# Loading and transposing one contraction block of x first, the next one behind the first weights, and moving one bank copy to VectorE

## The chip, the cores and the metric

The kernel runs on one core of a Trainium2 chip. The metric is device microseconds of one execution, so lower is better. A ratio below is always the mean time of one kernel's fast runs over the mean of the kernel before's fast runs of the same rounds on the same chip, with a 95% interval; it is therefore not quite the ratio of the medians that stand beside it. "By the clock" below means by these times; "the clock of TensorE" is the rate at which it works.

## The reference

```python
B, S, D, F = 32, 32, 1024, 3584        # bf16, x is 1024 tokens by 1024
def reference(x, w_gate, w_up, w_down):
    return (gelu(x @ w_gate) * (x @ w_up)) @ w_down     # tanh gelu
```

## The kernel before

A small recorder collects all operations, sorts those of each engine other than TensorE by an `at` value, works out the semaphores and emits five instruction streams. Most of the kernel (block products with sums of operands, Strassen-like) is not touched. What matters here is its first 12 us: the products of the first tokens with eight stripes of weights (four of gate, four of up), one contraction block of 128 at a time. TensorE needs x with the contraction on the partitions. Blocks 0 and 1 of x are loaded plainly and transposed by TensorE; later blocks come by transposing DMA.

```python
for n in [512] * 6 + [P] * 2:                      # warm-up matmuls, result unused
    mm(3, one[:, 0:P], one[:, 0:n], True, True)

NX = 2
for i, eng in enumerate(("sp", "act")):            # x, blocks 0 and 1 in one: rows of 512 B
    dma(eng, xn[:, 2 * i:2 * i + 2, :], x_r[:, 2 * i:2 * i + 2, 0:NX * P], 0, f"xn{i}")
# ...
for q in range(2):                                 # weights: gate on SP, up on ACT, block by block
    for k in range(NX):
        load_quad("sp", q, 0, k, k + 1)
        load_quad("act", q, 1, k, k + 1)
# ... transposing loads of x on SP, more weights on ACT ...
act(warm[:, 0:1], const0, GELU, 0)                 # brings the activation table in early
for k in range(NX):                                # eight transposes, four copies to SBUF
    for i, b in enumerate((6, 7) if k == 0 else (4, 5)):
        half = ps[:, b, 0:P].bitcast(BF16)
        for t in range(2):
            pr.add("pe", "transpose", half[:, t * P:(t + 1) * P], xn[:, 2 * i + t, k * P:(k + 1) * P], ident[:, :])
        pr.add("dve", "tensor_copy", xT[0][:, k, i * 256:(i + 1) * 256], half)
# ...
for k in range(NX):                                # first group: 8 products of block 0, 8 of block 1
    for j in range(2):
        for m in range(4):
            raw(m, j, k, 2 * m + j, k == 0)        # into PSUM bank 2m + j
            if k == NX - 1:                        # bank done: copied out, in turn by ScalarE and VectorE
                copy(("act", "dve")[m % 2], kept[m][:, j, :], bank(2 * m + j), 6.5 + 0.9 * j + 0.1 * m)
# ... the second group (m = 4 to 7) then fills the same eight banks, in the order 0 2 4 6 1 3 5 7
```

## Time and profile before

| | before |
|---|---|
| time, median of the first 3 runs | 271.86 us (271.35 to 272.02) |
| PE busy | 99% of the span |
| first product starts | 4.61 us |
| x lands (SP half, ACT half) | 3.25, 3.46 us |
| block-0 weights land (gate, up) | 4.03, 4.59 us |
| block-1 weights land (gate, up) | 6.74, 6.92 us |
| first product of block 1 | 7.32 us |
| first product of the second group | 9.04 us |

Landing times and starts of single matmuls are those recorded in the trace.

In the profile lines, PE is TensorE's matmuls, PEld its weight loads, DVE VectorE, ACT ScalarE and POOL GpSimd. `ps` is PSUM; `arena` holds the weights and transposed x; `hT` first holds x as loaded and later the copies of the banks. The page of the kernel before begins with the busy time of each engine:

```profile
PE 268.2 (99%) x1206; PEld 192.6 (71%) x1206; DVE 208.2 (77%) x246; ACT 136.1 (50%) x221; POOL 37.1 (14%) x23
```

The chain of waits of the kernel before, in order of time (start in us, length in us, what ran):

```profile
by line: PE ps L117 99.0%; DVE o L117 0.1%; issue 0.0%
...
0.77 3.79 PE ps L117 x16
4.56 0.05 issue
4.61 264.41 PE ps L117 x1190
...
```

The last line shown matters most: from 4.61 us on, 1190 matmuls follow one another and wait for nothing. What makes TensorE start later, do more, or wait once in the first microseconds is therefore added to the whole time.

The timeline of the kernel before up to 12.4 us, for TensorE, VectorE and ScalarE (start, length, engine, line, operation, output and inputs, count; in brackets the idle time before and what ended it):

```profile
0.77 2.93 PE L117 MATMUL ps<-const-bfloat16-1.0 128*128 128x512 bf16 x8 [0.77 <-PEq L632]
3.50 1.06 PE L117 MATMUL ps<-ident,hT 128*128 128x128 bf16 x8
4.61 8.05 PE L117 MATMUL ps<-arena 128*128 128x512 bf16 x32
...
3.95 0.93 DVE L117 COPY arena<-ps 128x256 bf16<-128x256 bf16 x4 [3.95 <-PE ps L117]
7.95 2.48 DVE L117 COPY hT<-ps 128x512 f32<-128x512 f32 x4 [3.06 <-PE ps L117]
...
5.25 1.28 ACT L117 ACT_TABLE_LOAD   x1 [5.25 <-issue]
7.73 1.57 ACT L117 ACTIVATE hT<-ps 128x512 f32<-128x512 f32 x3 [0.98 <-PE ps L117]
```

The warm-up lasts until 3.5 us, and x has just landed. All eight transposes follow at once. The products start when the first two copies are in SBUF. The copies that free the banks (output `hT`) are shared: four on VectorE, four on ScalarE. A matmul's own length overlaps with the next one's, so the pace has to be read from the starts: consecutive products of 512 columns start 0.427 us apart until 6.3 us and 0.216 us apart from 6.7 us on. The clock of TensorE doubled in between.

### The profile page before, as it was taken

What the parts mean: (1) busy time and instruction counts of PE and PEld (TensorE: products, weight loads), DVE (VectorE), ACT (ScalarE), POOL (GpSimd) and SP (SyncE); (2) the same over time, 40 slices, a digit from 0 to 9 for tenths busy, and PEclk for the clock granted to TensorE, in tenths of its full rate; (3) what the DMA queues carried; (4) which work ended last, traced back from release to release, by engine and by line L of the source; (5) the groups of instructions that cost most, each with busy time, mean ns of one, the idle gap of its engine ahead of it and who ended that gap; (6) DMA issues with size and microseconds to landing.
All of it is one profiled execution on the core that took longest, in us unless ns stands there. A gap on an engine that the chain in (4) does not pass through costs nothing.

```text
span 270.8 us, 3333 instructions
## 1 busy us (share of the span) xinstructions
PE 268.2 (99%) x1206; PEld 192.6 (71%) x1206; DVE 208.2 (77%) x246; ACT 136.1 (50%) x221; POOL 37.1 (14%) x23
## 2 busy tenths in 40 slices
PE   8999999999999999999999999999999999999997
PEld 4444448888888888888776776674458888888884
DVE  1338998998899889988764739379976999999921
ACT  2339877566756675667455554531220305057452
POOL 1000003123302330233344160000000000000000
DMA  6999970050492002971900070294010000002102
GB/s 205 205 316 204 280 188 4 13 141 0 116 291 60 0 0 80 254 251 51 263 0 0 0 247 27 65 351 129 0 39 19 4 0 0 0 0 80 58 21 97
DMA packets 45024, 27.47 MB, mean 101 GB/s; under 512 B 8656, under 2 KB 45008, under 8 KB 45008
## 3 DMA queue, kind: packets, MB, share of 16 engines
q1 hardware_dynamic: 42496, 25.04, 34.0%
q10 hardware_dynamic: 2512, 2.23, 3.3%
q8 instruction: 9, 0.15, 0.2%
q14 instruction: 7, 0.06, 0.1%
HBM read 23.33 MB, written 2.10 MB: 94 GB/s over the span
## 4 chain that ended last, share of the span: by engine, by line
PE 99%; DVE 0%; issue 0%
PE ps L117 99%; DVE o L117 0%
## 5 line engine op out<-in xcount | busy, mean ns | idle before, releaser
L117 PE MATMUL ps<-S,T 128*128 128x512 f32 x560 | 129.2, 391 | 0.0
L117 PEld LDWEIGHTS ps<-S,T 128*128 128x128 f32 x560 | 105.2, 188 | 22.3
L117 ACT ACTIVATE tmp<-ps 128x512 f32<-128x512 f32 x64 | 38.0, 596 | 51.7 <-PE ps L117 51.5
L117 POOL TENSOR_TENSOR T<-arena 128x1024 fp32r<-128x1024 bf16 x17 | 36.4, 2153 | 124.5 <-PE ps L117 81.7
L117 PE MATMUL ps<-T,S 128*128 128x512 f32 x224 | 51.3, 390 | 0.0
L117 DVE TENSOR_TENSOR T<-arena,T 128x1024 fp32r<-128x1024 bf16 x42 | 51.0, 1220 | 0.2
L117 PEld LDWEIGHTS ps<-T,S 128*128 128x128 f32 x224 | 42.1, 188 | 8.8
L117 ACT ACTIVATE ps<-ps 128x512 f32<-128x512 f32 x44 | 25.6, 584 | 37.0 <-PE ps L117 37.0
L117 DVE TENSOR_TENSOR hT<-tmp,ps 128x512 bf16<-128x512 f32 x56 | 37.0, 684 | 8.7 <-PE ps L117 6.7
L117 PE MATMUL ps<-arena 128*128 128x512 bf16 x192 | 43.5, 385 | 0.1
L117 DVE TENSOR_TENSOR tmp<-ps,tmp 128x512 f32<-128x512 f32 x28 | 19.4, 692 | 23.5 <-PE ps L117 23.5
L117 PEld LDWEIGHTS ps<-arena 128*128 128x128 bf16 x192 | 18.5, 99 | 23.7 <-issue 2.4
L117 DVE TENSOR_TENSOR T<-arena 128x1024 fp32r<-128x1024 bf16 x25 | 30.0, 1222 | 4.4 <-PE ps L117 4.3
L117 DVE TENSOR_TENSOR ps<-ps,tmp 128x512 f32<-128x512 f32 x32 | 22.3, 696 | 3.0 <-PE ps L117 3.0
L117 PE MATMUL ps<-arena,hT 128*128 128x512 bf16 (+2 forms) x126 | 24.6, 356 | 0.0
L117 PEld LDWEIGHTS ps<-arena,hT 128*128 128x128 bf16 x126 | 11.7, 98 | 12.7 <-issue 0.5
L117 ACT ACTIVATE tmp<-tmp 128x512 f32<-128x512 f32 x28 | 17.6, 632 | 2.4 <-DVE tmp L117 2.1
L117 ACT ACTIVATE ps<-hT 128x512 f32<-128x512 f32 x22 | 13.0, 599 | 7.6 <-DVE hT L117 7.6
L117 DVE TENSOR_TENSOR S<-hT 128x1024 fp32r<-128x1024 bf16 x14 | 16.6, 1221 | 0.0
L117 ACT ACTIVATE T<-arena 128x1024 fp32r<-128x1024 bf16 x14 | 14.8, 1059 | 0.0
L117 ACT ACTIVATE hT<-ps 128x512 f32<-128x512 f32 x18 | 9.5, 602 | 7.0 <-PE ps L117 7.0
L117 PE MATMUL ps<-S 128*128 128x512 f32 x56 | 12.9, 389 | 0.0
(33 smaller groups left out, 94.4 us busy)
## 6 DMA issues: line engine op xcount, KB each, us to landing
arena<-in_w_down_dram SPq DMA_DIRECT2D x4, 1792.0 KB, 9.4
arena<-in_w_gate_dram SPq DMA_DIRECT2D x10, 512.0 KB, 4.8
arena<-in_w_up_dram SPq DMA_DIRECT2D x10, 512.0 KB, 5.9
out_dram<-arena SPq DMA_DIRECT2D x12, 128.0 KB, 1.7
arena<-in_w_up_dram ACTq DMA_DIRECT2D x6, 128.0 KB, 5.6
arena<-in_w_gate_dram SPq DMA_DIRECT2D x3, 256.0 KB, 6.3
arena<-in_w_up_dram SPq DMA_DIRECT2D x3, 256.0 KB, 6.5
arena<-in_w_gate_dram SPq DMA_DIRECT2D x4, 128.0 KB, 5.1
```

What stands on the lines that cost most here:

```text
L117: ins = name(eng, *args, **kw) if callable(name) else getattr(eng, name)(*args, **kw)
```

## The change

The intent is to start sooner. x of block 0 is loaded alone, with half the bytes, then the first weights, then x of block 1, whose transposes run between the second and the third product. The diff also redistributes the eight copies: three on ScalarE, five on VectorE.

```diff
-        for i, eng in enumerate(("sp", "act")):
-            dma(eng, xn[:, 2 * i:2 * i + 2, :], x_r[:, 2 * i:2 * i + 2, 0:NX * P], 0, f"xn{i}")
+        def load_xn(k):
+            for i, eng in enumerate(("sp", "act")):
+                dma(eng, xn[:, 2 * i:2 * i + 2, k * P:(k + 1) * P], x_r[:, 2 * i:2 * i + 2, k * P:(k + 1) * P], 0, f"xn{k}{i}")
 ...
         for q in range(2):
             for k in range(NX):
+                if q == 0:
+                    load_xn(k)
                 load_quad("sp", q, 0, k, k + 1)
 ...
-        for k in range(NX):
-            for i, b in enumerate((6, 7) if k == 0 else (4, 5)):
-                half = ps[:, b, 0:P].bitcast(BF16)
+        def transposed(k):
+            for i in range(2):
+                half = ps[:, 5 + 2 * i if k else 6 + i, 0:P].bitcast(BF16)
 ...
+        transposed(0)
         for k in range(NX):
             for j in range(2):
                 for m in range(4):
+                    if (k, j, m) == (0, 0, 2):
+                        transposed(1)
                     raw(m, j, k, 2 * m + j, k == 0)
                     if k == NX - 1:
-                        copy(("act", "dve")[m % 2], kept[m][:, j, :], bank(2 * m + j), 6.5 + 0.9 * j + 0.1 * m)
+                        copy(("dve", "act")[(m, j) in ((3, 0), (0, 1), (3, 1))], kept[m][:, j, :], bank(2 * m + j), 6.2 + 0.9 * j + 0.1 * m)
```

## The prediction

> **What bounds the kernel.** TensorE: the page shows PE busy 99% and 99% of the chain of waits on PE. By the start times of consecutive matmuls in the timeline, PE never waits again once the first product has started at 4.61 us: products start 0.427 us apart until about 6.4 us and 0.216 us apart afterwards. So three things count: when the first product starts, TensorE's work before and after its clock doubles, and any new wait of TensorE in the first 12 us. Everything later shifts along.
>
> **The start before (timeline, landing times in the trace).** Warm-up matmuls run from 0.77 to 3.50 us. The two x loads (128 KB each) land at 3.25 and 3.46 us, just hidden by the warm-up. Eight transposes follow, 0.107 us each, until 4.35 us. The two block-0 copies on VectorE end at 4.25 and 4.46 us, and the first product starts 0.15 us later. The block-1 transposes run while PE would wait for these copies anyway. The first weights land at 4.03 and 4.59 us, those of block 1 at 6.74 and 6.92 us; block 1 starts at 7.32 us.
>
> **What the change does.**
> 1. x of block 0 is half the bytes and lands perhaps 0.3 to 0.5 us earlier. This buys nothing: the unchanged warm-up holds TensorE until 3.50 us, so the first product stays at about 4.6 us.
> 2. The four block-1 transposes move from a free gap to between products: 4 x 0.107 = 0.43 us. They run at the slow clock and what they delay partly at the fast one, so this costs 0.2 to 0.4 us. PE is idle some 0.7 us before the first product instead of 0.25.
> 3. x of block 1 now queues behind the first weights, in 256-byte rows rather than 512. The Trainium skill, "DMA: Bandwidth & Descriptors", section Specifications, gives 512 B as the minimum for line rate; here the 512-byte packets of x took about 28 ns and the 256-byte ones of the transposing loads about 26. It should land at 4.5 to 5.5 us, needed at 5.4; block-1 weights at 6.9 to 7.5 us, needed at 7.5. Estimated stall 0 to 0.8 us.
> 4. The eight copies that free the banks go from 4 on ScalarE + 4 on VectorE to 3 + 5. VectorE makes one per 0.60 us. Its third and fifth copies end about 0.2 and 0.5 us after the next products want their banks (before: 0.1 us of slack). Cost 0.3 to 0.6 us.
> 5. Two more DMA issues, 0.45 us each, one per queue, delay later loads by as much, within their slack of over 0.5 us.
>
> "TensorE: Matmul & The Clock Gate", Part 1, says the clock doubles after a busy window of 3.4 us that runs free. The trace agrees with its two rates. The longer idle gap could make one window count as not busy: about 1.7 us more, by my estimate with 15% chance.
>
> **Predicted:** 0.2 + 0.45 + 0.1 us, roughly: 272.6 us (before: 271.86), range 271.4 to 273.8. Chances: faster by over 2% 0.005, within 2% 0.985, slower 0.01.
>
> **What would show it.** First product at about 4.6 us; four 128-column matmuls after the second product; block 1 starting at about 7.5 us or later; waits of PE for VectorE at the banks near 10 and 11 us; no difference after 12 us.
>
> **What would make it wrong.** Runs in which x lands after the warm-up, so that the early half does start products earlier (up to 0.4 us gained); block-1 x landing late (a stall above 1 us); the clock staying slow another window.

## The result

| | before | after |
|---|---|---|
| median of 6 runs | 272.04 us (271.35 to 272.24) | 272.52 us (272.21 to 273.24) |
| ratio | | 1.0023 (1.0007 to 1.0039) |
| span of the profiled run | 270.8 us | 270.8 us |

The change makes the kernel a little slower, by about 0.6 us: the same by a margin of 2%, yet clear of the noise. A repeat later gave a median of 272.95 us and 1.0038 (1.0022 to 1.0053).

The two profiled spans are equal, which seems to contradict this. The profile after explains it. The page's first line and the chain of waits of the kernel after:

```profile
PE 267.5 (99%) x1206; PEld 191.9 (71%) x1206; DVE 208.9 (77%) x247; ACT 135.6 (50%) x220; POOL 37.1 (14%) x23
...
by line: PE ps L117 97.6%; DVE hT L117 1.1%; DVE arena L117 0.2%; issue 0.1%; DVE o L117 0.1%
0.77 3.16 PE ps L117 x10
...
3.96 0.52 DVE arena L117 x2
...
4.61 2.48 PE ps L117 x13
...
7.11 3.09 DVE hT L117 x5
...
10.25 258.69 PE ps L117 x1168
```

VectorE now stands on the chain twice. At 3.96 us it makes the two copies of transposed x, and TensorE has nothing to do meanwhile; the first product starts at 4.61 us, exactly as before. From 7.11 us it makes five copies in a row, and TensorE waits for the last of them. The 3.09 us of these five are not the loss, because TensorE worked during most of them. The loss is how much later the next matmul starts, as shown next.

The timeline of the kernel after over the same stretch:

```profile
0.77 2.93 PE L117 MATMUL ps<-const-bfloat16-1.0 128*128 128x512 bf16 x8 [0.77 <-PEq L641]
3.50 0.63 PE L117 MATMUL ps<-ident,hT 128*128 128x128 bf16 x4
4.61 0.59 PE L117 MATMUL ps<-arena 128*128 128x512 bf16 x2 [0.47 <-DVE arena L117]
5.04 0.39 PE L117 MATMUL ps<-ident,hT 128*128 128x128 bf16 x4
5.26 4.83 PE L117 MATMUL ps<-arena 128*128 128x512 bf16 x20
10.25 2.33 PE L117 MATMUL ps<-arena 128*128 128x512 bf16 x10 [0.16 <-DVE hT L117]
...
5.35 0.49 DVE L117 COPY arena<-ps 128x256 bf16<-128x256 bf16 x2 [0.89 <-PE ps L117]
7.11 3.08 DVE L117 COPY hT<-ps 128x512 f32<-128x512 f32 x5 [1.27 <-PE ps L117]
...
6.30 1.28 ACT L117 ACT_TABLE_LOAD   x1 [6.30 <-issue]
7.76 1.08 ACT L117 ACTIVATE hT<-ps 128x512 f32<-128x512 f32 x2
```

Two products go from 4.61 to 5.04 us, so they are 0.216 us apart: the clock was already fast at the first product, where before it was slow until past 6.3 us. That is worth 1.0 us, and most likely luck of the run (see the runs without a profile, below the ledger). It hides the three losses in this profile: four transposes take 0.22 us between products; block 1 waits 0.13 us for its gate weights, which land at 6.64 us; and the second group starts two of its matmuls 0.20 and 0.32 us late, at the banks that VectorE frees. "Idle before" shows only 0.16 us for the larger wait, since the modelled end of the preceding matmul covers the rest. The distance between starts is the measure.

### A ledger that all profiles share

From the first product of the second group's block 2 on, every profile needs the same time to its last matmul, 256.26 to 256.29 us. So the start of that product sums up all that happened earlier. It is worked out as: start of the first product, plus 32 products at 0.2159 us (6.91 us), plus what each distance between starts has above 0.2159 us, sorted by cause. The columns are: first product; time of transposes between products; excess of products at the slow clock; wait for block-1 gate weights; waits at the banks; the resulting start; and the landing of the block-1 gate weights.

| kernel | first | transposes | slow clock | weights | banks | start | gate-1 lands |
|---|---|---|---|---|---|---|---|
| before | 4.61 | 0 | 0.98 | 0 | 0 | 12.49 | 6.74 |
| before, repeated | 4.85 | 0 | 0.83 | 0 | 0 | 12.59 | 5.06 |
| before, copies 3 + 5 | 4.73 | 0 | 0.40 | 0 | 0.54 | 12.57 | 6.36 |
| before, late transposes | 4.61 | 0.43 | 0.81 | 0 | 0 | 12.75 | 6.59 |
| before, late transposes, copies 3 + 5 | 4.61 | 0.43 | 0.81 | 0 | 0.54 | 13.30 | 5.39 |
| before, x in two loads | 4.97 | 0 | 0.01 | 0 | 0.10 | 11.99 | 5.74 |
| before, short warm-up | 4.59 | 0 | 0.18 | 0 | 0 | 11.67 | 5.93 |
| before, long warm-up | 8.71 | 0 | 0 | 0 | 0 | 15.62 | 5.48 |
| after | 4.61 | 0.22 | 0.01 | 0.13 | 0.54 | 12.42 | 6.64 |
| after, repeated | 4.50 | 0.30 (0.08 of it a wait for x) | 0 | 0.21 | 0.54 | 12.47 | 6.68 |
| after, copies 4 + 4 | 4.61 | 0.22 | 0.01 | 0.50 | 0 | 12.24 | 7.01 |
| after, short warm-up | 4.18 | 0.43 | 0.68 | 0.36 | 0.54 | 13.10 | 7.32 |
| after, short warm-up, copies 4 + 4 | 4.18 | 0.43 | 0.61 | 0 | 0 | 12.13 | 6.62 |
| after, long warm-up | 8.63 | 0.22 | 0 | 0 | 0.54 | 16.30 | 6.51 |

Two columns are decided by the code: the banks cost 0.54 us in all six profiles with copies 3 + 5 and nothing with 4 + 4 (0.10 us in one), and transposes between products cost 0.22 us at the fast clock and 0.43 us at the slow one. In the repeat of the kernel after, the third transpose also waited 0.08 us for the ACT half of x of block 1, which landed at 5.06 us. The slow-clock column differs from run to run, by up to 0.98 us, about as much as all the rest together in the kernel after.

The runs without a profile help here. In all fourteen profiles the span less the start in the ledger is 258.3 to 258.4 us, so the start of any run can be estimated from its span. Of the 33 runs of the kernel before in the three later sets of rounds, 15 had a span of 269.8 or 269.9 us, hence a start near 11.5 us. That is 4.6 us plus the 6.91 us of the products, and leaves little room, 0.1 us or so, for a slow clock. The shortest of the 12 runs of the kernel after had 270.7 us, a start near 12.3 us. So, by this estimate, the kernel before often has the fast clock from its first product on too; its two profiles happened to be slow, and those of the kernel after fast. Fast against fast, the change costs about 0.9 us, which is what its three losses add up to (0.22, 0.13 and 0.54 us). No trace of these runs was kept.

### The profile page after: what moved, and what is told of

Same layout as the page of the kernel before. It is cut to its first block, busy times and chain, and to the rows that moved or that the text cites. A ratio compares the mean times of both kernels' runs of the same rounds, so it can differ in the third digit from the quotient of the medians.

```text
span 270.8 us, 3337 instructions
## 1 busy us (share of the span) xinstructions
PE 267.5 (99%) x1206; PEld 191.9 (71%) x1206; DVE 208.9 (77%) x247; ACT 135.6 (50%) x220; POOL 37.1 (14%) x23
## 3 DMA queue, kind: packets, MB, share of 16 engines
q10 hardware_dynamic: 2784, 2.23, 3.3%
## 4 chain that ended last, share of the span: by engine, by line
PE 98%; DVE 1%; issue 0%
PE ps L117 98%; DVE hT L117 1%; DVE arena L117 0%; DVE o L117 0%
```

## The experiments

### The two splits of the copies

The theory was that the 3 + 5 split of the copies is the main loss: VectorE makes one per 0.60 us, and its third and fifth come too late. The rival was that the transposes and loads cost the time and the copies nothing. First, the kernel after with the old copies:

```diff
-  copy(("dve", "act")[(m, j) in ((3, 0), (0, 1), (3, 1))], kept[m][:, j, :], bank(2 * m + j), 6.2 + 0.9 * j + 0.1 * m)
+  copy(("act", "dve")[m % 2], kept[m][:, j, :], bank(2 * m + j), 6.5 + 0.9 * j + 0.1 * m)
```

> The kernel after, with the eight bank-freeing copies back at 4 on ScalarE and 4 on VectorE in turn. Theory (the 3 + 5 split costs 0.5 us by making the next products wait for their banks): if the clock is still slow at the first products (block 1 starting at 7.5 us), ScalarE is ready in time, PE has no wait over 0.1 us at the banks and the time is about 0.5 us below the kernel after, ratio to before 1.000 to 1.001. If the clock is fast from the start (block 1 at 6.7 us), ScalarE is not done with its issues and its table load until 7.8 us, and PE waits for ScalarE instead, some 0.5 us in all: no gain, ratio 1.002. Rival (the copies don't matter, the moved transposes and the later loads cost the 0.6 us): ratio 1.002 whatever the clock, with no PE waits at the banks that add up to more than 0.2 us.

Measured: 271.92 us, ratio 1.0005 (0.9992 to 1.0019). There were no waits at the banks, although the clock was fast from the first product on. I had expected ScalarE to be late in that case. It was not, because block 1 itself started only at 7.05 us. The chain of waits of this run shows why:

```profile
2.23 4.78 DMA arena<-in_w_gate_dram
...
7.05 5.57 PE ps L117 x25
```

Block 1 waited for its gate weights, which had been issued at 2.23 us and took 4.78 us to land. The wait was 0.50 us.

Then the other way round, the kernel before with the new copies (the same edit reversed):

> The kernel before with nothing changed but the copies, 3 on ScalarE and 5 on VectorE as in the kernel after. Theory (copies): PE waits about 0.2 us for the third VectorE copy and 0.35 us for the fifth, in every run and at either clock, ratio 1.002. Rival (transposes and loads): those waits are absent or made good elsewhere, ratio 1.000.

Measured: 272.29 us, ratio 1.0017 (1.0005 to 1.0030), which is 0.46 us on 272 us. Its chain of waits has the same five copies as the kernel after:

```profile
4.73 2.52 PE ps L117 x9
...
7.27 3.09 DVE hT L117 x5
...
10.40 2.55 PE ps L117 x11
```

Alone, the copies cost 0.46 us by the clock (clear of zero) and 0.54 us in the trace. Taking them back from the kernel after gives about as much (1.0023 less 1.0005), but those two ratios come from different rounds and their intervals overlap. The rival in its strict form falls: the waits at the banks came and went with the copies.

### The warm-up: is the early half of x worth anything?

One of the six 512-column warm-up matmuls was taken out of each kernel:

```diff
-  for n in [512] * 6 + [P] * 2:
+  for n in [512] * 5 + [P] * 2:
```

> The kernel after with one 512-column warm-up matmul fewer (5 instead of 6), so that TensorE is free at 3.07 us when the early half of x is there (2.92 and 3.15 us). Theory (the warm-up, not x, held the first product at 4.61 us in the kernel after): first product at 4.2 to 4.35 us. What it brings in all depends on the clock: with a fast clock block 1 then waits for its weights at 6.8 us and nothing is gained; with a slow one 0.2 to 0.35 us. Ratio 1.000 to 1.003. Rival (something else, the identity or the copies, holds it): first product still at 4.6 us.

> The kernel before with the same shorter warm-up. Theory: x lands at 3.25 and 3.46 us, so the transposes start at 3.3 to 3.5 us whatever the warm-up does; first product between 4.5 and 4.75 us, ratio 0.999 to 1.001. Together with the run of the kernel after with the shorter warm-up it tells whether the early half of x has a value that the warm-up hides: rival is that both behave alike.

The timelines of TensorE, of the kernel after and then of the kernel before with the short warm-up:

```profile
4.18 1.01 PE L117 MATMUL ps<-arena 128*128 128x512 bf16 x2 [0.47 <-DVE arena L117]
...
7.37 3.41 PE L117 MATMUL ps<-arena 128*128 128x512 bf16 x14 [0.19 <-DMA arena<-in_w_gate_dram]
```

```profile
3.49 1.04 PE L117 MATMUL ps<-ident,hT 128*128 128x128 bf16 x8 [0.21 <-DMA hT<-in_x_dram]
4.59 7.68 PE L117 MATMUL ps<-arena 128*128 128x512 bf16 x34
```

In the kernel after, the first product started at 4.18 us instead of 4.61: the warm-up, not x, had held it. In the kernel before, the first half of x landed at 3.45 us, TensorE waited for it, and the first product stayed at 4.59 us. So the early half of x is real and hidden. But it brought nothing: 272.57 us, ratio 1.0024 (1.0010 to 1.0038) for the kernel after with the short warm-up, against 1.0003 (0.9985 to 1.0020) for the kernel before with it. In the profile, block 1 waited for its weights until 7.37 us and the copies cost their 0.54 us as always.

### One part at a time: transposes, and the loads

The kernel before with only the block-1 transposes moved (same loads, same copies):

```diff
 ... (the transposes become a function; those of block 1 use banks 5 and 7 instead of 4 and 5)
+  transposed(0)
   for k in range(NX):
       for j in range(2):
           for m in range(4):
+              if (k, j, m) == (0, 0, 2):
+                  transposed(1)
               raw(m, j, k, 2 * m + j, k == 0)
```

> The kernel before with one thing changed: the four block-1 transposes run between the second and third product, as in the kernel after; one load of x in 512-byte rows, as before. Theory (they leave a free gap and take PE's time): 0.22 us later at a fast clock, 0.43 at a slow one, unless block 1 waits for its weights anyway (they landed at 5.9 to 6.7 us in the runs of the kernel before and its variants, and PE alone would reach block 1 at 6.5 us at a fast clock); ratio 1.000 to 1.0015, first product at 4.6 to 4.75 us. Rival (the transposes are the larger part of the loss): ratio 1.002.

```profile
4.61 1.01 PE L117 MATMUL ps<-arena 128*128 128x512 bf16 x2 [0.47 <-DVE arena L117]
5.41 0.63 PE L117 MATMUL ps<-ident,hT 128*128 128x128 bf16 x4
5.84 6.43 PE L117 MATMUL ps<-arena 128*128 128x512 bf16 x27
```

Measured: 272.10 us, ratio 1.0024 (1.0012 to 1.0036). The interval reaches down to 0.33 us and the trace has 0.43 us (at the slow clock), so my band of up to 1.0015 was too low in the middle and the two meet only at the edge. The ratio is nearer the rival's 1.002 than the middle of my band. Which part is the larger stays open: by the clock the transposes (1.0024) and the copies (1.0017) can't be told apart, and in the traces the transposes are the smaller, 0.22 to 0.43 against 0.54 us.

The kernel before with only the x loads split, both halves still ahead of the weights:

```diff
-  dma(eng, xn[:, 2*i:2*i+2, :], x_r[:, 2*i:2*i+2, 0:NX*P], 0, f"xn{i}")
+  for k in range(NX):
+      dma(eng, xn[:, 2*i:2*i+2, k*P:(k+1)*P], x_r[:, 2*i:2*i+2, k*P:(k+1)*P], 0, f"xn{k}{i}")
```

> The kernel before with one thing changed: each x load is two, one per block, in 256-byte rows, still ahead of all weights; transposes and copies as before. Theory (the halved rows double the packets ahead of the block-1 weights, about 18 to 20 ns each against 28 for a 512-byte one, 512 more packets over 16 engines, so 0.3 us, and the two issues add up to 0.45 us each to every later load): the weights of block 1 land 0.3 to 0.7 us later than in the kernel before and near 7.0 us as in the kernel after, x of both blocks at 3.5 to 3.9 us, first product at 4.7 to 5.0 us; ratio 1.001 to 1.0025. Rival (landing times of the block-1 weights vary from run to run and the rows don't matter): weights at 5.9 to 6.7 us, ratio 1.000.

Measured: 272.03 us, ratio 1.0022 (1.0009 to 1.0035), in the expected band, but for a different reason. The block-1 gate weights landed at 5.74 us, early, so my theory that the short rows delay them falls here. What was late were the block-0 weights, gate at 4.92 us, as this chain of waits shows:

```profile
1.76 3.16 DMA arena<-in_w_gate_dram
...
4.97 263.52 PE ps L117 x1190
```

Whether it is the place of x of block 1 between the two blocks of weights that delays the block-1 weights stays open. The landing times differ between the groups (5.06 to 6.74 us in seven profiles with one load of x, mean 5.94; 6.51 to 7.32 us in six with block 1 behind the first weights, mean 6.80), and order is one thing that separates the groups. But the ranges overlap, and the block-1 gate load is also issued 0.5 us later in the second group (2.23 against 1.75 us); the split loads, issued at 2.26 us and landing at 5.74, speak against that as the cause, in one profile. No run isolates the mechanism.

Last, the kernel before with late transposes and copies 3 + 5, but the old loads:

> The kernel before with two of the change's three parts: block-1 transposes between the products and copies 3 + 5, but x in one load ahead of the weights. Theory (the three parts are mostly separate costs): bank waits of 0.20 and 0.32 us as with the copies alone, transposes between the products as with those alone, no earlier x; ratio 1.0025 to 1.005, at or above the kernel after, as the earlier first weights and x of the change gain little or nothing. Rival (the split loads are a cost of their own in the kernel after): ratio below that of the kernel after by 0.001 or more.

Measured: 272.81 us, ratio 1.0033 (1.0018 to 1.0048), and 0.54 us at the banks plus 0.43 us of transposes in the trace. The kernel after in the same rounds had 1.0038, in the first ones 1.0023. So with these two parts in place the new order of the loads neither gains nor loses anything that these rounds can resolve. Against that, the kernel after with copies 4 + 4 had 1.0005 and the kernel before with late transposes 1.0024, which would give the new loads a gain of 0.5 us. The two comparisons differ by about what their intervals allow, and I draw no figure from them.

### No DMA to wait for

With 20 warm-up matmuls instead of 6, everything has landed and the clock is fast before the first product:

```diff
-  for n in [512] * 6 + [P] * 2:
+  for n in [512] * 20 + [P] * 2:
```

> The kernel after with 20 warm-up matmuls of 512 columns instead of 6, so that all of x and of the weights of both blocks have landed before the first product and the clock is fast by then: no DMA is waited for. Theory: transposes between products 0.22 us and bank waits 0.20 + 0.32 us show in the trace, in all about 0.75 us above the kernel before with the same warm-up. Rival (the loss comes from the DMA order): the two agree within 0.3 us.

> The kernel before with the same 20 warm-up matmuls. Theory: no wait of PE after the first product, block 1 starts 1.73 us after the first product, the next group another 1.73 us later; total 2.5 to 4 us above the kernel before, and 0.75 us below the kernel after with the same warm-up.

The timelines of TensorE, of the kernel before and then of the kernel after with this warm-up:

```profile
7.77 0.61 PE L117 MATMUL ps<-ident,hT 128*128 128x128 bf16 x8
8.71 7.50 PE L117 MATMUL ps<-arena 128*128 128x512 bf16 x34 [0.34 <-DVE arena L117]
```

```profile
8.63 0.59 PE L117 MATMUL ps<-arena 128*128 128x512 bf16 x2 [0.56 <-DVE arena L117]
9.06 0.39 PE L117 MATMUL ps<-ident,hT 128*128 128x128 bf16 x4
9.29 4.69 PE L117 MATMUL ps<-arena 128*128 128x512 bf16 x20
14.13 2.12 PE L117 MATMUL ps<-arena 128*128 128x512 bf16 x9 [0.16 <-DVE hT L117]
```

From the first product to the end of the ledger the first takes 6.90 us and the second 7.67 us: 0.77 us more, where 0.75 was expected, made of 0.22 us of transposes and 0.54 us at the banks. With the long warm-up the kernel after has a ratio of 1.0163 (1.0147 to 1.0178) and the kernel before one of 1.0145 (1.0132 to 1.0158), with means of 275.89 and 275.41 us. The 0.48 us between them are not clear of noise, as each interval is some 0.4 us to either side; the doubling, now within the warm-up (near 5.8 and 6.0 us), still moves the first product. In the traces, with neither the DMA nor the slow clock in the way after the first product, the two losses remain.

### The kernel after, mended

> The kernel after with its avoidable losses mended: one warm-up matmul fewer, and copies 4 + 4. Theory: first product at 4.2 us, no bank wait over 0.1 us, but block 1 still starts no earlier than its weights land, 6.6 to 7.3 us, and the transposes still take PE's time, so it only comes level with the kernel before: ratio 0.999 to 1.001. Rival (the early half of x is worth its 0.4 us once the warm-up and the copies don't hide it): ratio 0.9985 or less.

This is the kernel after with five warm-up matmuls and copies 4 + 4 (both edits shown above). Measured: 271.92 us, ratio 1.0007 (0.9993 to 1.0021). The timeline of TensorE:

```profile
3.07 0.63 PE L117 MATMUL ps<-ident,hT 128*128 128x128 bf16 x4
4.18 1.01 PE L117 MATMUL ps<-arena 128*128 128x512 bf16 x2 [0.47 <-DVE arena L117]
4.99 0.63 PE L117 MATMUL ps<-ident,hT 128*128 128x128 bf16 x4
5.41 6.88 PE L117 MATMUL ps<-arena 128*128 128x512 bf16 x30
```

The first product is 0.43 us earlier, and the transposes between the products take 0.43 us. That is the whole account at the slow clock. The expected rival, a gain of the early half of x (0.9985 or less), lies below the interval. No version here beats the kernel before.

### Both kernels again

> The kernel before, word for word, for a second profile and a measure of what noise does. Theory (its slow first products are a matter of when the clock doubles, which differs from run to run): first product at 4.6 to 4.75 us, no wait at the banks, block 1 anywhere from 6.4 to 7.5 us, with weights of block 1 at 5.9 to 6.9 us; ratio 0.999 to 1.001, runs between 271.3 and 272.3 us. Rival (the clock doubles at a fixed time): 6.4 us again, as in the first profile.

> The kernel after, word for word. Theory: bank waits of 0.20 and 0.32 us again, first product at 4.6 us again, weights of block 1 at 6.6 to 7.3 us, the clock doubling at some other time; ratio 1.0015 to 1.003. Rival (the first profile's waits were chance): other waits, or none.

The kernel before came to 272.03 us, ratio 1.0007 (0.9992 to 1.0022) to itself, which is what the noise does; the medians of the kernel before in the three sets of rounds were 271.99, 271.40 and 271.75 us. The kernel after came to 272.95 us and 1.0038, with 0.20 and 0.32 us at the banks again; the ratio lies above the 1.0015 to 1.003 that I had expected. In the repeat of the kernel before x landed late, at 3.72 and 3.94 us, as its chain of waits shows:

```profile
0.74 2.98 DMA hT<-in_x_dram
...
3.77 1.04 PE ps L117 x8
...
4.85 8.12 PE ps L117 x33
```

Here TensorE did wait for x, and the first product came at 4.85 us, later than expected; the block-1 gate weights landed at 5.06 us, earlier than expected. In the kernel after and its copies variant, x of block 0 landed by 3.22 us and the first product was never later than 4.61 us. So the early half of x is worth 0.24 us in such a run. The doubling of the clock did not settle the rival as neatly as I had hoped: the two profiles of the unchanged kernel before have it at nearly the same time, 6.3 to 6.8 us. Over all fourteen profiles it lies between about 3.45 us (the kernel before with split loads) and 6.7 us, so it isn't fixed. The kernel before with copies 3 + 5, which differs from the kernel before only after 7 us, has it at about 5.6 us. But among the profiles with six warm-up matmuls, all four with x in two loads have the fast clock at the first product and none of the five with one load does. The short spans of the kernel before (below the ledger) speak for chance, not for the loads, but no trace settles it.

## Why the prediction was right

The measured median of 272.52 us lies beside the predicted 272.6 us, and the sum was right for mostly the right terms. That it lies within 0.1 us is luck: the prediction added 0.75 us to a median of 271.86 us, which after six runs was 272.04; the ratio has an interval from 0.2 to 1.1 us, and fast against fast the cost is nearer 0.9.

1. The early half of x "buys nothing": right in the profile, where the first product started at 4.61 us in both kernels, and confirmed with the shorter warm-up. It is not right for every run. Where x lands late, it is worth up to 0.24 us. The prediction named this as a way to be wrong.
2. Moved transposes, 0.2 to 0.4 us: 0.22 us at the fast clock and 0.43 at the slow one. The part alone measured 0.65 us by the clock, with an interval from 0.33 us up.
3. x of block 1 landing at 4.5 to 5.5 us: 4.67 and 4.86 us, and TensorE didn't wait for it; in the repeat, 4.87 and 5.06 us, and a wait of 0.08 us. The larger wait that came was for the block-1 weights, 0.13 and 0.21 us in the two profiles (about 0.1 in the sum). I had put them at 6.9 to 7.5 us and needed at 7.5; they landed at 6.64 us and were needed sooner.
4. Copies, 0.3 to 0.6 us, 0.45 in the sum: 0.54 us in every profile, 0.46 us by the clock when changed alone.
5. Later loads: nothing to see. The rest of the kernel takes the same 256.3 us.

What was wrong was the start of block 1 "at about 7.5 us or later": it was at 6.68 us. That number took the clock of the profile before as given, slow until 6.4 us. In the profile after the clock was fast at the first product, which made up 1.0 us and left two equal spans of 270.8 us. The feared extra slow window after the longer idle gap did not show in its two profiles: in the first the gap from the last transpose's start to the first product's start was 0.79 us (3.82 to 4.61), and the clock was fast at its end.

## What to carry to other kernels

When one engine is busy without a break from some early point on, write a ledger of its starts up to that point; every part of a change then has its own column, and the clock of TensorE, which differs from run to run, has its own too, so that two profiles of equal span can be seen to differ by several opposite amounts. Moving work "later, between the products" is only a gain if what is freed earlier was what the products waited for; here the earlier slot was a free gap. And when copies free the buffers of the next group, count each engine's copies against the order in which the buffers are wanted, because the last copy of the busier engine sets the wait: here VectorE's five, 0.60 us apart, ended at 10.20 us, when the bank of the fifth had been wanted at 9.93 us (the start of the next product less its wait).

## What the Trainium skill lacked or had wrong

- "TensorE: Matmul & The Clock Gate", Part 1, gives about 3.4 us of sustained activity before the clock doubles, with a window that runs free. The two rates agree (0.427 and 0.216 us per 512 columns). In these runs the doubling came between about 2.7 and 5.9 us after the first matmul at 0.77 us, so in two profiles (2.7 and 2.8 us) sooner than a full window of work. A span of 3.3 us in the onset moved this kernel's ledger by up to 1.0 us; the page's "<1% of a typical kernel span" holds (0.4%), but that is more than the effect under study, and two single profiles can differ by it.
- "DMA: Bandwidth & Descriptors", Specifications, asks for 512 B at least. On the ACT queue the 512-byte packets of x took 30.0 ns on average in the kernel before, the 256-byte ones 18.0 ns in the kernel after: 17 against 14 bytes per ns and engine. (In other profiles with one load of x they took 27.0 ns.) The loss is there but mild. The page describes in which order queues and engines work; I found no page that gives the time which a load put ahead costs a later one. Here the same 128 KB load landed between 5.06 and 7.32 us.
- "Perfetto Trace Analysis", Identifying the Most-Contended Engine, says that the busy share of matmuls is no good measure of how near a kernel is to the roofline. It couldn't tell the two kernels apart here either: PE is 99% busy in both. What that section does not add is that the idle time before a matmul can be understated, where the modelled end of the one before lies too late: a matmul that started 0.32 us late shows 0.16 us of idle.
